# Two-layer transformer block on one core: one buffer for both feed-forward weights, reloaded per chunk, ten more probability tiles, and two scheduler constants raised

## The chip, the cores and the metric

The kernel runs on one core of one Trainium2 chip. The metric is the device time of one execution in microseconds. Every kernel was run several times, and one more execution was profiled. Engines are named as the profile names them: PE is TensorE, PEld its weight loads, DVE VectorE, ACT ScalarE, POOL GpSimd, SP SyncE with the DMA queue.

## The reference

Two attention layers (32 heads of 16) and two feed-forward layers (512 to 1376 to 512) alternate over 2,048 tokens; both attention layers use the same weights, and so do both feed-forward layers.

```python
x = A_x
x = x + _A_ref(_layernorm(x, axis=-1), A_wqkv, A_wo)
x = x + _B_ref(_layernorm(x, axis=-1), B_w1, B_b1, B_w2, B_b2)
x = x + _A_ref(_layernorm(x, axis=-1), A_wqkv, A_wo)
x = x + _B_ref(_layernorm(x, axis=-1), B_w1, B_b1, B_w2, B_b2)
# _A_ref: scores = q k^T * Dh^-0.5; p = softmax(scores); (p v) @ wo
# _B_ref: layernorm; gelu(y @ w1 + b1) @ w2 + b2
```

## The kernel before

The program is a list scheduler. Jobs written as generators hand it tasks, and when the kernel is built, a small time model in the program decides in which fixed order each engine gets its instructions. Every constant of that model can thus change the order of all that follows; this matters below.

Score tiles of 128 keys by 512 queries are made in groups, alternately three and two banks of PSUM, the memory that TensorE writes its results to. ScalarE turns a group into probabilities (exp) in slots of the tile `PT`, and a group cannot be issued before it has a slot:

```python
pl["pt3"] = Pool([0, 3, 6])     # three slots of three tiles
pl["pt2"] = Pool([9, 11])       # two slots of two tiles
...
ptn = "pt3" if gi % 2 == 0 else "pt2"
self.starved = not S_.pools[ptn].free
if self.starved:
    self.try_pv()
pt = yield ("get", ptn)
```

Some tiles go to VectorE instead, which makes exp by adding an offset to the bits (`dp`, called D tiles in the code), two tiles to a batch, with three shifted copies. A D tile needs four PV products (probabilities times V) where a ScalarE tile needs one. No new batch begins while DFLY are in flight:

```python
if self.batch is None and (not S_.pools["dp"].free or S_.pools["dp"].waiters or self.flying >= DFLY):
    return None
```

PV products are put together in bursts of one or two passes, four heads side by side. A burst is issued if its value reaches PV_LEAST, if a score group is starved for a slot, or at a segment's end (a segment is one group of four heads with one chunk of queries and a range of keys; all segments share one PSUM accumulator bank):

```python
value = lambda r: sum(min(r, len(v)) for v in by.values()) / (4.0 * (r + PV_COST))
r = max(range(1, PV_DEEP + 1), key=value)
if value(r) < PV_LEAST and not self.starved and len(near) < sg["n"] - sg["sub"]:
    return
```

The first chunk of each layer is split in two parts by keys, so that attention can begin before all keys are there. In the second layer these are eight segments of 48 tiles and eight of only 16; the segments of later full chunks have 64. Both feed-forward weights lie in buffers of their own and are loaded once, after which the key ("wld",) is marked and the small bias job starts:

```python
def bias():
    yield ("keys", [("wld",)])
    b = yield ("get", "mb")                       # takes a PSUM bank
    yield Task("pe", 3.0, [...transpose of the bias...])
    yield Task("dve", 3.0, [...copy out of the bank...])   # 3.0: a late priority
    S_.release("mb", b)
```

## Time and profile before

| | before |
|---|---|
| median time | 1733.0 us (4 runs, 1721.7 to 1734.5) |
| ScalarE busy | 1616.2 us of the 1733.2 us span |
| ScalarE exp (L1065) | 1541.0 us, 3,340 tiles |
| TensorE PV products (L1233) | 650.0 us |
| score tiles to VectorE (L1150) | 756 |
| ScalarE idle from 900 to 1120 us, the change of layers | 22.4 us |

The idle time of a stretch is its length less ScalarE's busy time in it. The prediction shows the lines.

### The profile page before, as it was taken

The numbers are of one execution on the slowest core, as the hardware profiler recorded it, in microseconds if no ns is written. First come the engines' busy times: TensorE is split into PE (matmuls) and PEld (weight loads), VectorE is DVE, ScalarE is ACT, GpSimd is POOL, SyncE is SP. The second block draws the span as 40 slices with busy tenths as digits, with TensorE's granted clock in tenths as the row PEclk, the third lists the DMA queues.
The fourth block names the chain that finished last, engine by engine and source line by source line (L and its number), as shares of the span: only waits on it lengthen the run. The fifth ranks groups of instructions, "written<-read, shape, count | busy, mean of one in ns | idle before, by whom it ended". The sixth has DMA issues, their size and how long they took to land.

```text
span 1733.2 us, 45114 instructions
## 1 busy us (share of the span) xinstructions
PE 1623.7 (94%) x19139; PEld 594.5 (34%) x19278; DVE 1383.1 (80%) x2994; ACT 1616.2 (93%) x1427; POOL 382.9 (22%) x640
## 2 busy tenths in 40 slices
PE   8989999999999999999999999999999999999998
PEld 5223323333233323233333333323233233344455
DVE  6778988868878688868888799886898879886674
ACT  3889999999999999999989898899999999999995
POOL 4145531102211122101112123411111101222310
PEclk9899999999999999999999999999999999999999
DMA  6462000001100020101541111010000100010000
GB/s 162 90 147 83 15 9 8 20 4 38 48 16 11 5 59 29 19 5 29 107 69 23 26 48 19 14 19 8 16 8 7 20 15 5 6 19 7 19 13 11
DMA packets 146446, 55.35 MB, mean 32 GB/s; under 512 B 131047, under 2 KB 140104, under 8 KB 146248
## 3 DMA queue, kind: packets, MB, share of 16 engines
q1 hardware_dynamic: 146248, 52.46, 13.9%
q8 instruction: 154, 2.52, 0.6%
q14 instruction: 44, 0.36, 0.1%
HBM read 8.69 MB, written 15.30 MB: 14 GB/s over the span
## 4 chain that ended last, share of the span: by engine, by line
PE 55%; ACT 28%; DVE 11%; issue 2%; POOL 2%; DMA 1%; DVEq 0%; POOLq 0%; another core or an unknown queue 0%; SPq 0%
ACT PT L1065 25%; PE ps L1233 18%; PE ps L1082 17%; PE ps L990 5%; PE ps L797 4%; DVE dp L1150 4%; PE ps L1351 3%; PE ps L1386 3%; DVE dp L1178 3%; PE ps L1319 3%; ACT h L1379 2%; DVE accT L1259 1%; PE ps L993 1%; POOL vs L941 1%; DMA xnT<-xn 1%
## 5 line engine op out<-in xcount | busy, mean ns | idle before, releaser
L1065 ACT ACTIVATE PT<-ps 128x1536 bf16<-128x1536 f32 (+1 forms) x1349 | 1541.0, 1258 | 84.1 <-PE ps L1082 73.9
L1150 DVE TENSOR_SCALAR dp<-ps 128x512 uint16<-128x512 f32 x756 | 511.5, 684 | 222.5 <-PE ps L1082 214.9
L1082 PE MATMUL ps<-QT,KT 32*128 32x512 bf16 (+1 forms) x4608 | 588.7, 362 | 66.0 <-DVE dp L1150 28.1
L1233 PE MATMUL ps<-PT,V 128*17 128x512 bf16 (+1 forms) x3762 | 548.2, 361 | 0.0
L941 POOL TENSOR_SCALAR vs<-V 128x340 bf16<-128x340 bf16 (+3 forms) x312 | 256.4, 828 | 916.0 <-PE ps L1233 875.4
L1178 DVE TENSOR_SCALAR dp<-dp 128x1024 uint16<-128x1024 uint16 (+1 forms) x1155 | 448.2, 433 | 4.3
L1233 PE MATMUL ps<-dp,vs 128*17 128x512 bf16 (+1 forms) x2538 | 440.2, 360 | 1.7 <-DVE dp L1178 1.7
L1082 PEld LDWEIGHTS ps<-QT,KT 32*128 32x128 bf16 x4608 | 156.4, 91 | 566.6 <-issue 211.7
L990 PE MATMUL ps<-wqkv,zw 128*32 128x256 bf16 x5864 | 256.2, 279 | 1.1 <-DVE accT L1259 1.1
L1233 PE MATMUL ps<-dp,V 128*17 128x512 bf16 (+1 forms) x846 | 213.8, 361 | 7.8 <-DVE accT L1259 6.8
L1233 PEld LDWEIGHTS ps<-PT,V 128*17 128x17 bf16 x3762 | 137.4, 88 | 136.5 <-issue 113.6
L990 PEld LDWEIGHTS ps<-wqkv,zw 128*32 128x32 bf16 x5864 | 151.2, 97 | 70.0 <-issue 48.2
L1233 PEld LDWEIGHTS ps<-dp,vs 128*17 128x17 bf16 x2538 | 118.0, 89 | 129.3 <-issue 96.5
L797 PE MATMUL ps<-wqkv,xnT 128*128 128x512 bf16 x298 | 90.0, 395 | 10.8 <-DMA xnT<-xn 5.1
L1351 PE MATMUL ps<-yT,w 128*128 128x512 bf16 (+3 forms) x361 | 91.1, 356 | 6.2 <-issue 2.9
L1386 PE MATMUL ps<-w,h 128*128 128x512 bf16 x269 | 73.2, 381 | 4.3 <-issue 3.7
L1373 DVE TENSOR_SCALAR h<-ps,b1c 128x512 bf16<-128x512 f32 (+2 forms) x88 | 62.0, 705 | 18.9 <-PE ps L1351 18.5
L1259 DVE STREAM_TRANSPOSE accT<-ps 128x512 f32<-128x512 f32 (+1 forms) x88 | 58.0, 659 | 19.0 <-PE ps L1233 13.7
L1233 PEld LDWEIGHTS ps<-dp,V 128*17 128x17 bf16 x846 | 52.0, 89 | 50.9 <-issue 19.1
L1319 PE MATMUL ps<-wo,OT 128*128 128x512 bf16 x213 | 58.9, 381 | 4.2 <-issue 3.7
L1299 DVE STREAM_TRANSPOSE OT<-ob 128x512 bf16<-128x512 bf16 (+1 forms) x72 | 46.0, 640 | 0.2
L1351 PEld LDWEIGHTS ps<-yT,w 128*128 128x128 bf16 (+1 forms) x396 | 29.5, 99 | 43.7 <-issue 18.1
(148 smaller groups left out, 747.4 us busy)
## 6 DMA issues: line engine op xcount, KB each, us to landing
q_scr<-qk SPq DMA_DIRECT2D x22, 256.0 KB, 2.0
k_scr<-qk SPq DMA_DIRECT2D x12, 256.0 KB, 2.0
out_dram<-xres SPq DMA_DIRECT2D x16, 128.0 KB, 1.7
v_scr<-vst SPq DMA_DIRECT2D x12, 136.0 KB, 1.9
V<-v_scr SPq DMA_DIRECT2D x8, 204.0 KB, 4.9
wqkv<-in_A_wqkv_dram SPq DMA_DIRECT2D x3, 512.0 KB, 5.1
q_scr<-h SPq DMA_DIRECT2D x6, 256.0 KB, 2.3
qraw<-q_scr SPq DMA_TRANSPOSE x87, 2.6
```

Source lines behind the costliest of these rows:

```text
L797: yield Task("pe", prio, [I(lambda e, c=c: e.matmul(self.ps[:, b, :], lhsT=xnT[:, c, :], rhs=self.wqkv[:, c, which * 512:which * 512 + 512 ...
L941: yield Task("pool", 0.8, [I(lambda e, k=k: e.tensor_scalar(out=self.vs[:, q, k - 1, i:i + n, :], in0=src, scalar1=WSHIFT[k], scalar2=None ...
L990: P.op("pe", lambda e, p=p: e.matmul(self.ps[p:p + 32, b, 0:w], lhsT=self.zw[:, 0:32], rhs=rhs[:, 0:w], start=st, stop=st, skip_group_chec ...
L1065: S_.submit(Task("act", 1e-5 * gi, [I(lambda e, pt=pt, n=n, b0=b0: e.activation(out=self.PT[:, pt:pt + n, :], in_=self.ps[:, b0:b0 + n, :] ...
L1082: return [I(lambda e, kb=kb, i=i: e.matmul(self.ps[:, b, i * W:(i + 1) * W], lhsT=self.KT[32 * hp:32 * hp + 32, hg, kb * 128:(kb + 1) * 12 ...
L1150: self.S_.submit(Task("dve", 0.0, [I(lambda e: e.tensor_scalar(out=self.dp[:, u, w * 512:(w + 1) * 512], in0=self.ps[:, b, :], scalar1=BIT ...
L1178: yield Task("dve", pr, [I(lambda e, k=k, v=v: e.tensor_scalar(out=self.dp[:, v, 0:N], in0=self.dp[:, u, 0:N], scalar1=float(SHIFT[k]), sc ...
L1233: ops.append((i, I(lambda e, hp=hp, v=v, ap=ap[:, i * W:(i + 1) * W], first=first and i == 0, W=W: e.matmul(self.ps[32 * hp:32 * hp + 17, ...
L1259: yield Task("dve", 0.3, [I(lambda e: e.transpose(self.accT[:, a, 0:W], self.ps[:, ACCB, 0:W]), [("ps", ACCB)], [RA], 0.15 + 0.53 * W / 512)])
L1319: yield Task("pe", pr, [I(lambda e, hg=hg, i=i, b=b: e.matmul(self.ps[:, b, :], lhsT=self.OT[:, hg, i * 128:(i + 1) * 128], rhs=self.wo[:, ...
L1351: yield Task("pe", pr, [I(lambda e, c=c: e.matmul(self.ps[0:M, b, off:off + W], lhsT=self.w1[:, c, fc * 128:fc * 128 + M], rhs=self.yT[:, ...
L1386: yield Task("pe", pr, [I(lambda e, fc=fc, i=i, b=b: e.matmul(self.ps[:, b, :], lhsT=self.gt(fc, i, W), rhs=self.w2[:, fc, :], start=(fc = ...
```

## The change

The intent: keep only one of the two feed-forward weights on the chip at a time, reload both for each chunk of tokens, and use the freed space for probability slots, so that exp can run further ahead and PV products can wait until full bursts of eight are together. In the second layer the second weights lie in the buffer of the QKV weights, which are no longer needed then.

```diff
-DFLY = 3
+DFLY = 4
...
-PV_LEAST = 0.6
+PV_LEAST = 0.75
...
-        self.w1 = t("w1", [128, 4, self.F], BF16)
-        self.w2 = t("w2", [128, NFC, 512], BF16)
+        self.wf = t("wf", [128, NFC, 512], BF16)
...
-        self.PT = t("PT", [128, 13, 512], BF16)
+        self.PT = t("PT", [128, 23, 512], BF16)
...
-        pl["pt3"] = Pool([0, 3, 6])
-        pl["pt2"] = Pool([9, 11])
+        pl["pt3"] = Pool([0, 3, 6, 13, 18])
+        pl["pt2"] = Pool([9, 11, 16, 21])
...
-            (the loads of w1 and w2 in the start-up job)
             S_.mark(("wld",))
...
+        yield ("keys", [("kv", 1, tt) for tt in range(self.NT)] + [("wld",)])
+        for qc in range(self.NC + 1):
+            L = 1 if qc < self.NC else 3
+            if qc:
+                yield ("keys", [("post", 1, qc - 1)])
+            for fc in range(self.NFC):
+                yield first(fc)
+                S_.mark(("w1", L, qc % self.NC, fc))
+            if L == 1:
+                for fc in range(self.NFC):
+                    yield ("keys", [("w1u", 1, qc, fc)])
+                    yield from second(1, fc)
+                    S_.mark(("w2", 1, qc, fc))
... (matmuls and waits take the new names; the second layer loads both weights once)
```

More of the change, by code (lines that the diff above doesn't have):

```diff
@@ L687, in fills @@
             yield f(lambda e: e.memset(self.bst[:, :], 0.0), [("bst",)], 0.3)
-            yield f(lambda e: e.memset(self.w2[:, nfull, :], 0.0), [("w2z",)], 0.6)
+            yield f(lambda e: e.memset(self.wf[:, nfull, :], 0.0), [("wf", nfull)], 0.6)
             yield f(lambda e: e.memset(self.g10[:, :], 0.0), [("g10",)], 0.6)
@@ L699, in fills @@
                 yield ld(lambda e, hp=hp: e.dma_start(self.wo[32 * hp:32 * hp + 16, :, :], wor[hp]), [("wo0",)], [("wo", hp)])
-            w1r = self.B_w1.rearrange("(c p) n -> p c n", p=128)
-            for c in range(4):
-                yield ld(lambda e, c=c: e.dma_start(self.w1[:, c, :], w1r[:, c, :]), [], [("w1", c)])
-            w2r = self.B_w2[0:nfull * 128, :].rearrange("(c p) n -> p c n", p=128)
-            for c in range(0, nfull, 5):
-                yield ld(lambda e, c=c: e.dma_start(self.w2[:, c:c + 5, :], w2r[:, c:c + 5, :]), [], [("w2", c // 5)])
-            yield ld(lambda e: e.dma_start(self.w2[0:self.FLAST, nfull, :], self.B_w2[nfull * 128:self.F, :]), [("w2z",)], [("w2", 2)])
-            yield ld(lambda e: e.dma_start(self.w2[96:97, nfull, :], self.B_b2.rearrange("(o n) -> o n", o=1)), [("w2z",)], [("w2", 3)])
             S_.mark(("wld",))
         S_.spawn(fills(), 4.0)
+        S_.spawn(self.flow_weights(), 2.0)
         def bias():
@@ L717, in build_startup_late, with w1, w2, w2res @@
         S_.spawn(bias(), 3.0)
+    def w1(self, fc, c):
+        M = 128 if fc < self.NFC - 1 else self.FLAST
+        return self.wf[:, fc, c * M:(c + 1) * M]
+    def w2(self, L, fc):
+        if L == 1:
+            return self.wf[:, fc, :]
+        return self.wqkv[:, :, :].rearrange("p c n -> p (c n)")[:, fc * 512:(fc + 1) * 512]
+    def w2res(self, L, fc):
+        return [("wf", fc)] if L == 1 else [("w2", fc)]
+    def flow_weights(self):
+        S_ = self.S_
+        nf = self.NFC - 1
+        wr1 = self.B_w1.rearrange("(c p) n -> p c n", p=128)
+        ld = lambda fn, writes: self.dma(fn, [], writes, 2.0, 0.1, 4.0)
+        def first(fc):
+            M = 128 if fc < nf else self.FLAST
+            dst = self.wf[:, fc, 0:4 * M].rearrange("p (c m) -> p c m", m=M)
+            return ld(lambda e: e.dma_start(dst, wr1[:, :, fc * 128:fc * 128 + M]), [("wf", fc)])
+        def second(L, fc):
+            W = self.w2res(L, fc) + ([("wqkv", fc % 3)] if L == 3 else [])
+            M = 128 if fc < nf else self.FLAST
+            yield ld(lambda e: e.dma_start(self.w2(L, fc)[0:M, :], self.B_w2[fc * 128:fc * 128 + M, :]), W)
+            if fc == nf:
+                yield ld(lambda e: e.dma_start(self.w2(L, fc)[M:M + 1, :], self.B_b2.rearrange("(o n) -> o n", o=1)), W)
+        yield ("keys", [("kv", 1, tt) for tt in range(self.NT)] + [("wld",)])
[6 more added lines that the diff above has]
+                S_.mark(("w1", L, qc % self.NC, fc))
+            if L == 1:
+                for fc in range(self.NFC):
+                    yield ("keys", [("w1u", 1, qc, fc)])
+                    yield from second(1, fc)
+                    S_.mark(("w2", 1, qc, fc))
+        yield ("keys", [("kd", 3, tt) for tt in range(self.NT)])
+        for fc in range(self.NFC):
+            yield from second(3, fc)
+            S_.mark(("w2", 3, 0, fc))
+        for qc in range(1, len(self.units[3])):
+            for fc in range(self.NFC):
+                S_.mark(("w1", 3, qc, fc))
+                S_.mark(("w2", 3, qc, fc))
     def ln_group(self, tiles, slot, prio, eps1, eps0):
@@ L837, in job_qkv_tile @@
             S_.release("mb", b)
+        S_.mark(("kd", L, tt))
         if not start:
@@ L1346, in job_yt, with mm_w1 @@
         S_.mark(("yt", L, tt))
-    def mm_w1(self, fc, b, pr, W, off=0):
+    def mm_w1(self, L, qc, fc, b, pr, W, off=0):
         M = 128 if fc < self.NFC - 1 else self.FLAST
+        yield ("keys", [("w1", L, qc, fc)])
         for c0 in (0, 2):
-            yield Task("pe", pr, [I(lambda e, c=c: e.matmul(self.ps[0:M, b, off:off + W], lhsT=self.w1[:, c, fc * 128:fc * 128 + M], rhs=self.yT[:, c, 0:W], start=(c == 0), stop=(c == 3)),
-                                    [("w1", c)] + [("yT", i) for i in range(W // 128)], [("ps", b)], 0.216 * W / 512, [("ps", b)]) for c in (c0, c0 + 1)])
+            yield Task("pe", pr, [I(lambda e, c=c: e.matmul(self.ps[0:M, b, off:off + W], lhsT=self.w1(fc, c), rhs=self.yT[:, c, 0:W], start=(c == 0), stop=(c == 3)),
+                                    [("wf", fc)] + [("yT", i) for i in range(W // 128)], [("ps", b)], 0.216 * W / 512, [("ps", b)]) for c in (c0, c0 + 1)])
     def gt(self, fc, i, W):
@@ L1369, in job_ffn @@
             M = 128 if fc < nf else self.FLAST
-            yield ("ready", "pe", [("yT", i) for i in range(len(tiles))])
+            yield ("keys", [("w1", L, qc, fc)])
+            yield ("ready", "pe", [("yT", i) for i in range(len(tiles))] + [("wf", fc)])
             b = yield ("get", "mb")
-            yield from self.mm_w1(fc, b, pr, W)
+            yield from self.mm_w1(L, qc, fc, b, pr, W)
+            S_.mark(("w1u", L, qc, fc))
             S_.submit(Task("dve", pr - 0.7, [I(lambda e, fc=fc, M=M, b=b: e.tensor_scalar(out=hv[0:M, fc * W:(fc + 1) * W], in0=self.ps[0:M, b, 0:W], scalar1=self.b1c[0:M, fc:fc + 1], scalar2=None, op0=ALU.add),
@@ L1381, in job_ffn @@
         GR = HR + [("g10",)]
+        yield ("keys", [("w2", L, qc, fc) for fc in range(NFC)])
         for i, tt in enumerate(tiles):
-            yield ("ready", "pe", GR)
+            yield ("ready", "pe", GR + [r for fc in range(NFC) for r in self.w2res(L, fc)])
             b = yield ("get", "mb")
             for f0 in range(0, NFC, 2):
-                yield Task("pe", pr, [I(lambda e, fc=fc, i=i, b=b: e.matmul(self.ps[:, b, :], lhsT=self.gt(fc, i, W), rhs=self.w2[:, fc, :], start=(fc == 0), stop=(fc == nf)),
-                                        GR + [("w2", k) for k in range(4)], [("ps", b)], 0.216, [("ps", b)]) for fc in range(f0, min(f0 + 2, NFC))])
+                yield Task("pe", pr, [I(lambda e, fc=fc, i=i, b=b: e.matmul(self.ps[:, b, :], lhsT=self.gt(fc, i, W), rhs=self.w2(L, fc), start=(fc == 0), stop=(fc == nf)),
+                                        GR + self.w2res(L, fc), [("ps", b)], 0.216, [("ps", b)]) for fc in range(f0, min(f0 + 2, NFC))])
             S_.submit(Task("dve", pr - 0.7, [I(lambda e, tt=tt, b=b: e.tensor_tensor(out=self.xres[:, tt, :], in0=self.ps[:, b, :], in1=self.xres[:, tt, :], op=ALU.add), [("ps", b), ("x", tt)], [("x", tt)], 0.68)]),
@@ L1425, in second @@
             GR = [("gt", fc)]
-            yield Task("pe", pr - 0.1, [I(lambda e, i=i: e.matmul(self.ps[:, acc[i], :], lhsT=self.gt(fc, i, W), rhs=self.w2[:, fc, :], start=(fc == 0), stop=(fc == nf)),
-                                          GR + [("w2", k) for k in range(4)], [("ps", acc[i])], 0.216, [("ps", acc[i])]) for i in range(n)])
+            yield ("keys", [("w2", L, qc, fc)])
+            yield Task("pe", pr - 0.1, [I(lambda e, i=i: e.matmul(self.ps[:, acc[i], :], lhsT=self.gt(fc, i, W), rhs=self.w2(L, fc), start=(fc == 0), stop=(fc == nf)),
+                                          GR + self.w2res(L, fc), [("ps", acc[i])], 0.216, [("ps", acc[i])]) for i in range(n)])
             if fc == nf:
@@ L1436, in job_tail @@
             b = yield ("get", "mb")
-            yield from self.mm_w1(fc, b, pr, W)
+            yield from self.mm_w1(L, qc, fc, b, pr, W)
             dst = self.gv[:, fc * W:(fc + 1) * W] if fc < nf else self.g10[0:M, 0:W]
```

## The prediction

> **What bounds the kernel now.** I read the page's engine table first, then the slices, the costliest groups (also with the shapes kept apart), the table of stretches, and last a few microseconds of the timeline.
>
> ```profile
> PE 1623.7 (94%) x19139; PEld 594.5 (34%) x19278; DVE 1383.1 (80%) x2994; ACT 1616.2 (93%) x1427; POOL 382.9 (22%) x640
> L1065 ACT ACTIVATE PT<-ps 128x1536 bf16<-128x1536 f32 (+1 forms) x1349 | 1541.0, 1258 | 84.1 <-PE ps L1082 73.9
> L1150 DVE TENSOR_SCALAR dp<-ps 128x512 uint16<-128x512 f32 x756 | 511.5, 684 | 222.5 <-PE ps L1082 214.9
> L990 PE MATMUL ps<-wqkv,zw 128*32 128x256 bf16 x5864 | 256.2, 279 | 1.1 <-DVE accT L1259 1.1
> ```
>
> PE's 94% is not a bound: the group on L990, 5,864 matmuls, is filler put into gaps to keep the clock up (its result is used nowhere). ScalarE is. Its exp group alone is 1541.0 us, and only 84.1 us of idle time stand before it. The table of stretches shows how little is left:
>
> ```profile
> 0.00:125.00 125.00, 112.19 (x930) 45.10 (x941) 87.32 (x207) 83.33 (x91) 44.00 (x122) 0.89 0.61 134
> 200.00:900.00 700.00, 660.25 (x7196) 221.85 (x7256) 562.31 (x1190) 678.61 (x586) 129.25 (x184) 0.99 0.14 30
> 900.00:1120.00 220.00, 206.06 (x2491) 73.99 (x2497) 192.54 (x415) 197.60 (x176) 65.50 (x121) 0.98 0.12 26
> 1120.00:1680.00 560.00, 529.63 (x7015) 201.56 (x7061) 452.44 (x986) 550.56 (x473) 100.17 (x95) 1.00 0.06 12
> 1680.00:1734.00 54.00, 46.55 (x697) 27.82 (x705) 21.75 (x50) 34.89 (x38) 1.52 (x4) 1.00 0.03 11
> ```
>
> The fourth busy column is ScalarE: 678.61 of 700 and 550.56 of 560. Of its 117 us idle, 42 lie before 125 us and 19 after 1680 us (start and tail, which the change doesn't touch); 22 lie from 900 to 1120, where the second attention layer waits for the first one's feed-forward part; some 35 are small gaps elsewhere. So the time can fall in two ways: those gaps, or fewer tiles for ScalarE. The second exists because a score tile (128x512) can go either to ScalarE, or to VectorE, which makes exp by bit arithmetic (one eviction on L1150, then three shifted copies on L1178, two tiles to a copy), at the price of four PV products in place of one.
>
> Unit costs. ScalarE: 642 groups of three tiles and 707 of two are 3,340 tiles, 1541.0 / 3340 = 0.461 us each. VectorE, for a tile of its own: 684 ns plus 3 x 438 / 2 ns = 1.34 us (438 ns is the mean of the 1024-wide copies with shapes kept apart). VectorE is 80% busy and waits 214.9 us for scores to evict, so it has room.
>
> **What the Trainium skill says.** "ScalarE: Activation LUTs", What ACT_TABLE_LOAD costs: an ACTIVATE with immediate scale and bias takes 186 ns + 0.833 N, and back-to-back ones overlap by 93 ns. For N = 1536 and 1024 that is 1466 and 1039 ns; the trace has 1482 and 1054. So exp runs at its floor, and buffers cannot make a tile cheaper. "TensorEngine Tiling (Array Packing)", Key Properties: changing the tiling mode drains TensorE. Scores are row-tiled and PV products column-tiled, so each PV burst pays it. The trace agrees:
>
> ```profile
> 702.86 0.09 PEld L1233 LDWEIGHTS ps<-PT,V 128*17 128x17 bf16 x1 [0.23 <-issue]
> ...
> 703.18 0.10 PEld L1082 LDWEIGHTS ps<-QT,KT 32*128 32x128 bf16 x3 [0.23 <-PE ps L1082]
> ...
> 704.94 0.09 PEld L1233 LDWEIGHTS ps<-dp,V 128*17 128x17 bf16 x1 [0.23 <-DVE dp L1150]
> ...
> 705.50 0.13 PEld L1082 LDWEIGHTS ps<-QT,KT 32*128 32x128 bf16 x3 [0.46 <-PE ps L1082]
> ```
>
> A burst of one pass (four products side by side) occupies 0.32 us from its start to the next scores, one of two passes 0.56 us: 0.08 us fixed and 0.24 us a pass. "DMA: Bandwidth & Descriptors", Specifications: transfers under 512 B miss line rate. The new first-weight loads come in 256-byte rows; no run yet shows what that costs.
>
> **The change part by part.** The instruction order is fixed when the program is built, so its decisions, though not their times, can be counted from the kernel before. I counted them: 1,574 PV bursts, 1,056 of one pass and 518 of two, 545 of them forced because no probability slot was free; 403 of the 1,349 score groups met an empty slot pool, 387 of these the pool of two slots; and 208 times a new VectorE batch was refused because three were in flight, in 187 of which a PSUM bank was free.
>
> *PV_LEAST 0.6 to 0.75.* The value of a burst is (tiles) / 4(r + 0.5) with r passes. One full pass is 0.67, two passes with six, seven and eight tiles are 0.6, 0.7 and 0.8. So only full bursts of eight pass now, apart from forced ones and ends of segments. *Ten more tiles* (five slots of three and four of two, from three and two) are what allows waiting for eight. Today's 3,340 + 4 x 756 = 6,364 PV tiles need 796 full bursts; with an odd one for each of 88 segments, some 900 of about 1,720 passes. Saved on TensorE: 670 x 0.08 + (2,092 - 1,720) x 0.24 = 143 us. Nearly all lies beside ScalarE and will turn into filler and idle time. What pays is a score group that no longer comes late. Outside start and tail ScalarE idles 57 us; the 22 us of the layer transition are mostly data not yet computed, so I take about a quarter: 15 us.
>
> *DFLY 3 to 4.* The 187 refusals bring far fewer new batches: a refusal with three in flight mostly means that VectorE is behind with its copies, and the next try a microsecond later succeeds. One in eight, two tiles each, is about 45 more tiles. On VectorE, 45 x 1.34 = 60 us, beside the path (to about 85%). TensorE gets 135 more PV tiles, 34 passes, 8 us, paid from the 143. ScalarE loses 45 x 0.461 = 21 us, on the path.
>
> *Shared weight buffer.* It frees 128x4x1376 bf16, 11,008 B a partition, for ten tiles of 1,024 B. It adds some 107 DMA issues and 11.3 MB (five loads of 2.8 MB in place of one), against 55.35 MB now and a mean DMA load of 32 GB/s. First weights are reloaded once the chunk before is through, about a chunk's attention (some 190 us) ahead; second weights when their column's first product is issued, behind the rest of those products, a 4.5 us gelu and table loads, against 4 to 6 us to landing for today's weight loads. Hidden; I count 0.
>
> Sum: 1733.9 - 15 - 21 = 1698; I say 1697 us.
>
> **Rivals.** *Only ScalarE's floor.* If no more tiles go to VectorE, at most small gaps close: 1715 to 1728, same. For it: 98% busy from 1120 to 1680 us. Against: the refusals counted, and VectorE's 215 us of waiting. *VectorE fills up.* If most refusals turn into batches, 110 more tiles put VectorE at 1383 + 147 = 1530 us, still below the span, and save 51 us; with 20 us of gaps, 1663. Against: the refusals come when it is behind; and 708 other refusals, for want of a PSUM bank, remain. *Large bursts block scores.* A burst holds TensorE 0.56 us, and a two-tile exp lasts about 0.95 us, of which the next scores need some 0.4 with their wait. If 850 bursts cost 0.04 us each, 34 us are lost and the gain is gone: 1730. For it: ScalarE waits on scores already; against: 518 two-pass bursts run today at 97% ScalarE. *Weights come late.* A stall of 4 us in the chunk from 900 to 1120 us, the one on the path, or a reload held up in the in-order DMA queue, adds 4 to 10 us, no more, since the other chunks' feed-forward runs beside attention.
>
> **Range and chances.** The centre is 36 us below, almost exactly the 2% line (1699). The floor rival and the blocking rival pull up, the VectorE rival down. 80%: 1662 to 1727. Faster by over 2%: 0.52; within 2%: 0.44; slower: 0.04, since no part of it puts more than some 10 us on the path.
>
> **What would show it.** PV: unbroken runs of L1233 matmuls, 1,100 now at a mean of 6.5, fall below 900. L1150 rises from 756 to about 800 and L1065's busy time falls by about 20 us to 1520. ScalarE's idle time between 125 and 1680 us falls from 57 to about 42. Filler on L990 rises above 5,864. VectorE goes to about 85%. No wait on a weight load appears among the longest. Wrong if L1150 stays at 756, if ScalarE's idle time before L1065 grows (blocking), or if feed-forward matmuls wait for DMA.

## The result, and the profile after

The changed kernel took 1707.5 us in the median (4 runs, 1704.4 to 1710.4) against 1733.0 us; all runs were fast ones. Ratios are the mean time of one kernel's fast runs over that of the other's of the same rounds, so they are not quite the ratio of the medians: here 0.9866, with a 95% interval from 0.9819 to 0.9913. Repeated later beside other kernels it was 0.9891 (0.9871 to 0.9911). The time lies in the predicted range, but the gain is 1.1 to 1.3%, not 2.1%.

One figure has to be held beside every comparison below: the granted TensorE clock that each run lists. In each kernel's own fast runs the time goes with it (correlation -0.88 to -0.99), by 1.0 to 1.5 us for each 0.001; the 54 runs of the kernel before in the last rounds reach from 1741.6 us at 0.982 to 1721.7 us at 0.993. The traces show the clock at 0.50 in short stretches, often 3.4 or 6.8 us long, and at 1.00 between them. The changed kernel's median clock in its repeat was 0.9835, that of the kernel before 0.989. At the same clock the gain is thus larger: at 0.985 one run of 1705.7 us stands against 1734.7 and 1736.5 us. What lowers the clock was not tested.

The engine table and the costliest groups of the profile after (line, engine and operation, count, busy time and mean, idle time before):

```profile
PE 1585.4 (93%) x19711; PEld 568.6 (33%) x19711; DVE 1374.4 (80%) x3011; ACT 1609.6 (94%) x1426; POOL 378.5 (22%) x640
L1110 ACT ACTIVATE PT<-ps 128x1536 bf16<-128x1536 f32 (+1 forms) x1348 | 1534.3, 1262 | 67.0 <-PE ps L1127 61.3
L1195 DVE TENSOR_SCALAR dp<-ps 128x512 uint16<-128x512 f32 x758 | 510.2, 682 | 208.4 <-PE ps L1127 200.7
L1035 PE MATMUL ps<-wqkv,zw 128*32 128x256 bf16 x6152 | 241.5, 280 | 1.1 <-DVE accT L1304 1.1
```

L1110 answers to L1065 of before, L1195 to L1150, L1035 to L990. VectorE got 758 tiles for 756, so nothing moved away from ScalarE. What fell is the idle time before exp, from 84.1 to 67.0 us, and with it the busy time, by 6.7 us, though a group's mean did not shorten. The span fell by 24.6 us: 18.0 us less idle time on ScalarE and 6.6 us less busy time.

The table of stretches says where (columns as before: after the stretch come PE, PEld, DVE, ACT and POOL busy, clock and DMA):

```profile
200.00:900.00 700.00, 657.02 (x7644) 214.17 (x7640) 566.01 (x1216) 682.99 (x593) 125.72 (x184) 0.99 0.18 42
900.00:1120.00 220.00, 202.48 (x2473) 69.93 (x2465) 189.73 (x414) 209.40 (x188) 67.18 (x123) 0.99 0.19 46
1120.00:1680.00 560.00, 524.60 (x7529) 201.26 (x7530) 454.99 (x999) 549.53 (x474) 97.53 (x92) 0.99 0.06 13
```

From 900 to 1120 us ScalarE is busy for 209.40 us where it was for 197.60; the two long stretches change by 4.4 and -1.0 us. Counted by exp tiles instead of time, the changed kernel is 7.5 us ahead at its 1,700th tile (which before ended at 884 us) and 22.8 us ahead at its 2,100th (1,100 us); after that it only keeps its lead.

The waits of ScalarE around that stretch (895 to 1120 us; engine and what it waited for, us in total, times, longest), first before, then after:

```profile
ACT PT L1065 <- PE ps L1082: 22.9, 20, 3.6
```

```profile
ACT PT L1110 <- PE ps L1127: 9.5, 18, 1.8
```

One of the waits of before, in the order of time (start, duration, engine and line):

```profile
1078.93 1.48 PE L1233 MATMUL ps<-PT,V 128*17 128x512 bf16 x7
...
1080.20 1.06 PE L1233 MATMUL ps<-dp,vs 128*17 128x512 bf16 x2
...
1081.20 1.03 PE L1082 MATMUL ps<-QT,KT 32*128 32x512 bf16 x5
...
1081.87 2.37 ACT L1065 ACTIVATE PT<-ps 128x1024 bf16<-128x1024 f32 x2 [3.60 <-PE ps L1082]
```

Here a new segment could only begin its PV products once the accumulator of the last one had been read (the transpose on L1259, from 1077.53 us for 0.71 us); those products ran from 1078.5 to 1081.3 us, the next scores started at 1081.20, and exp had sat idle for 3.60 us. This wait, the longest of the stretch, is not a clean example, since the clock was 0.50 from 1075.8 to 1082.6 us. But it does not stand alone. Of the waits of exp over 0.25 us from 900 to 1120 us, 21.6 us in all, eight with 15.8 us end within 4 us after an accumulator was read, seven of them at full clock; after, it is six with 6.3 us of 7.9 us. From 200 to 900 us, with 28 such reads to the 16 here, the same count gives 2.5 us before and 1.0 us after. Reading the schedule as it was built, 57 of the 163 groups of these sixteen short segments found their slot pool empty before, and 16 of 167 after. Over the whole kernel it was 403 of 1,349 and 66 of 1,348.

TensorE's busy time on PV products (the table of stretches with that line alone) fell as predicted, though the time hardly did. Before:

```profile
0.00:1734.00 1734.00, 650.00 (x7146) 179.08 (x7146) 0.99 0.15 32
```

After:

```profile
0.00:1709.00 1709.00, 521.52 (x7179) 136.36 (x7179) 0.98 0.17 39
```

The first figure after the stretch is PE: 128.5 us less for much the same products (7,179 recorded for 7,146; the schedule has only six PV tiles more, and some records are missing).

### The profile page after: what moved, and what is told of

It is laid out like the page before. It is cut to its first block, busy times and chain, and to the rows that moved or that the text cites. A ratio compares the mean times of both kernels' runs of the same rounds, so it can differ in the third digit from the quotient of the medians.

```text
span 1708.6 us, 46394 instructions
## 1 busy us (share of the span) xinstructions
PE 1585.4 (93%) x19711; PEld 568.6 (33%) x19711; DVE 1374.4 (80%) x3011; ACT 1609.6 (94%) x1426; POOL 378.5 (22%) x640
## 4 chain that ended last, share of the span: by engine, by line
PE 47%; ACT 40%; DVE 8%; POOL 2%; issue 2%; DMA 1%; SPq 0%; DVEq 0%; POOLq 0%
ACT PT L1110 37%; PE ps L1127 15%; PE ps L1278 13%; PE ps L1035 4%; PE ps L841 4%; PE ps L1397 4%; DVE dp L1195 3%; PE ps L1364 3%; PE ps L1435 3%; ACT h L1427 2%; DVE dp L1223 2%; POOL vs L986 1%; DVE accT L1304 1%; PE ps L1038 1%; ACT L1110 1%
## 5 line engine op out<-in xcount | busy, mean ns | idle before, releaser
L1110 ACT ACTIVATE PT<-ps 128x1536 bf16<-128x1536 f32 (+1 forms) x1348 | 1534.3, 1262 | 67.0 <-PE ps L1127 61.3
L1127 PE MATMUL ps<-QT,KT 32*128 32x512 bf16 (+1 forms) x4608 | 604.2, 363 | 108.5 <-ACT PT L1110 43.8
L1195 DVE TENSOR_SCALAR dp<-ps 128x512 uint16<-128x512 f32 x758 | 510.2, 682 | 208.4 <-PE ps L1127 200.7
L1278 PE MATMUL ps<-PT,V 128*17 128x512 bf16 (+1 forms) x3751 | 469.7, 363 | 0.4 <-DVE accT L1304 0.4
L1278 PE MATMUL ps<-dp,vs 128*17 128x512 bf16 (+1 forms) x2571 | 397.3, 359 | 0.0
L1035 PE MATMUL ps<-wqkv,zw 128*32 128x256 bf16 x6152 | 241.5, 280 | 1.1 <-DVE accT L1304 1.1
L1278 PE MATMUL ps<-dp,V 128*17 128x512 bf16 (+1 forms) x857 | 201.4, 364 | 3.0 <-DVE accT L1304 2.9
L1035 PEld LDWEIGHTS ps<-wqkv,zw 128*32 128x32 bf16 x6152 | 144.5, 97 | 93.3 <-issue 76.0
L1278 PEld LDWEIGHTS ps<-PT,V 128*17 128x17 bf16 x3751 | 114.7, 88 | 91.1 <-issue 73.7
L1278 PEld LDWEIGHTS ps<-dp,vs 128*17 128x17 bf16 x2571 | 101.9, 89 | 85.3 <-issue 71.4
L1397 PE MATMUL ps<-yT,wf 128*128 128x512 bf16 (+3 forms) x396 | 98.5, 359 | 0.5 <-DVE h L1421 0.3
L906 POOL TENSOR_TENSOR qt<-n,qy 128x32 f32<-128x32 f32 x32 | 11.1, 347 | 160.1 <-DVE qy L902 159.6
L1397 PEld LDWEIGHTS ps<-yT,wf 128*128 128x128 bf16 (+1 forms) x396 | 29.5, 99 | 46.5 <-issue 18.6
```

The source lines that it names most:

```text
L1035: P.op("pe", lambda e, p=p: e.matmul(self.ps[p:p + 32, b, 0:w], lhsT=self.zw[:, 0:32], rhs=rhs[:, 0:w], start=st, stop=st, skip_group_chec ...
L1110: S_.submit(Task("act", 1e-5 * gi, [I(lambda e, pt=pt, n=n, b0=b0: e.activation(out=self.PT[:, pt:pt + n, :], in_=self.ps[:, b0:b0 + n, :] ...
L1127: return [I(lambda e, kb=kb, i=i: e.matmul(self.ps[:, b, i * W:(i + 1) * W], lhsT=self.KT[32 * hp:32 * hp + 32, hg, kb * 128:(kb + 1) * 12 ...
L1195: self.S_.submit(Task("dve", 0.0, [I(lambda e: e.tensor_scalar(out=self.dp[:, u, w * 512:(w + 1) * 512], in0=self.ps[:, b, :], scalar1=BIT ...
L1278: ops.append((i, I(lambda e, hp=hp, v=v, ap=ap[:, i * W:(i + 1) * W], first=first and i == 0, W=W: e.matmul(self.ps[32 * hp:32 * hp + 17, ...
L1397: yield Task("pe", pr, [I(lambda e, c=c: e.matmul(self.ps[0:M, b, off:off + W], lhsT=self.w1(fc, c), rhs=self.yT[:, c, 0:W], start=(c == 0 ...
```

## The experiments

The questions: is it the slots, the bursts, DFLY, or the reload that does it; and where do the slots pay? The first four kernels do one part alone or undo one, with five rounds each, beside the kernel before (1727.9 us in these rounds, 19 runs).

**Weights only (e1).** The changed kernel, with all other parts undone:

```diff
-DFLY = 4
+DFLY = 3
-PV_LEAST = 0.75
+PV_LEAST = 0.6
-        pl["pt3"] = Pool([0, 3, 6, 13, 18])
-        pl["pt2"] = Pool([9, 11, 16, 21])
+        pl["pt3"] = Pool([0, 3, 6])
+        pl["pt2"] = Pool([9, 11])
```

> The changed kernel with only the shared, reloaded weight buffer left of it: five probability slots, DFLY 3 and PV_LEAST 0.6 as before. If the reload is hidden, as predicted: within 0.4% of before, 1727 to 1740 us, and the second layer's start (900 to 1120 us) as idle on ScalarE as before, about 22 us. If the reload itself is what brings part of the gain, or costs: below 1725 or above 1742 us.

Measured: 1749.3 us, 1.0112 of before (1.0089 to 1.0134). That was a miss: the reload seemed to cost 19 us. But the stretch at the change of layers is as before (22.6 us idle). The loss is one gap. The timeline of this kernel from 103 to 137 us:

```profile
104.01 0.17 PE L706 MATMUL ps<-ident,bst 32*128 32x32 bf16 x1
...
134.73 0.15 DVE L707 CAST b1c<-ps 128x11 f32<-128x11 bf16 x1
134.92 0.63 PE L1127 MATMUL ps<-QT,KT 32*128 32x512 bf16 x7
135.37 2.37 ACT L1110 ACTIVATE PT<-ps 128x1024 bf16<-128x1024 f32 x2 [29.41 <-PE ps L1127]
```

The bias is transposed into a PSUM bank at 104.01 us, and its copy out of the bank, at the late priority 3.0, comes 30.7 us later. As the copy ends, seven score matmuls start, and exp ends a gap of 29.41 us. In the code, the first score groups of five banks wait until each bank has been given up by the small jobs. The changed kernel marks ("wld",) before the large loads, not after them, so the bias job now starts just when those banks are being collected. In the kernel before, its transpose ran at 129.1 us, when that was over, and took 3.0 us with its copy.

**Slots only (e2).** As e1, but with the ten tiles and their slots.

```diff
-DFLY = 4
+DFLY = 3
-PV_LEAST = 0.75
+PV_LEAST = 0.6
```

> Shared weights and the ten tiles more, but DFLY 3 and PV_LEAST 0.6. Buffer theory (the slots let exp run on over the ends of segments, most where these are short, at the start and at the change of layers): nearly the whole gain, 1705 to 1715 us, ScalarE idle from 900 to 1120 us at most 13 us. Burst theory (it is TensorE time saved by large bursts that pays): at most a third of the gain, 1724 us or more.

Measured: 1732.8 us, 1.0018 of before (1.0003 to 1.0034). By its time this is the burst theory's case (1724 us or more), but the time decides nothing, since this kernel has the same gap as e1 (29.3 us, its bias copy 30.6 us late). It is 16.5 us faster than e1, and idles 17.8 us from 900 to 1120 us, where the buffer theory said at most 13.

**DFLY undone (e3).** The changed kernel with `DFLY = 3`.

> The changed kernel with DFLY 3. Counted in its schedule, 747 tiles go to VectorE in place of 758. If DFLY 4 brings these 11 tiles and no more: 11 x 0.461 = 5 us slower than the changed kernel, about 1712 us. If it does nothing: 1707 us. If it carries the gain: 1720 us or more.

Measured: 1719.8 us, 0.9948 of before (0.9929 to 0.9967). Half of the gain is gone, nearly the 1720 us set for "it carries the gain" and more than eleven tiles explain (747 went to VectorE, as counted). Its idle time at the change of layers is 15.4 us. The last experiment shows why this difference may not be read as DFLY's worth.

**Bursts only (e4).** The kernel before with `PV_LEAST = 0.75`.

> The kernel before with PV_LEAST 0.75 and nothing else. Counted in its schedule, bursts fall only from 1574 to 1393, and those forced by want of a slot rise from 545 to 962. Burst theory: some gain, 1715 to 1725 us. Buffer theory: none, since a pool of five slots can't wait for eight; 1730 to 1745 us.

Measured: 1749.4 us, 1.0105 of before (1.0078 to 1.0131): no gain, and somewhat worse than the buffer theory said. Larger bursts without slots make exp wait: from 900 to 1120 us ScalarE is busy for 188.79 us, so it idles 31.2 us there.

In the second four the two bias instructions got early priorities, so that the gap of e1 cannot hide the rest (before: 1727.4 us in these rounds, 55 runs):

```diff
-            yield Task("pe", 3.0, [...transpose of the bias...])
-            yield Task("dve", 3.0, [...copy out of the bank...])
+            yield Task("pe", 0.3, [...transpose of the bias...])
+            yield Task("dve", -1.0, [...copy out of the bank...])
```

**Weights only, bias mended (e5).** e1 with this edit.

> The weights-only kernel of the first four runs, with only the priority of the two bias instructions raised (their transpose and its copy out of a PSUM bank). There the copy came 30.7 us after its transpose and held a bank that the five-bank score groups waited for: one idle gap of 29.4 us on ScalarE. Bias theory (the reload itself costs nothing, the late copy of its earlier-freed bias job does): the gap goes to about 6 us, the time to 1.0112 - 23/1728 = 0.998 of before, about 1724 us. Rival (the reload's DMA costs the 19 us): still above 1742 us.

Measured: 1734.8 us, 1.004 of before (1.0025 to 1.0055), between the numbers of the two theories (1724 us, and over 1742). The waits from 95 to 140 us, in e1 and then here:

```profile
ACT PT L1110 <- PE ps L1127: 31.1, 3, 29.4
```

```profile
ACT PT L1110 <- PE ps L1127: 11.5, 5, 8.8
```

The gap went from 29.4 to 8.8 us and the copy follows its transpose after 0.8 us. The median fell by 14.5 us, the profiled span by 22.3 (the profiled run of e1 was its slowest, at a clock of 0.985; that of e5 had 0.991). So the late copy is the larger part of e1's loss; what stays, 0.4%, is within what a new order of instructions does by itself (see the last experiment), and no trace shows a feed-forward matmul that waits for weights.

**Slots only, bias mended (e6).** e2 with this edit.

> The pool-only kernel with the same two priorities raised. Bias theory: 1.0018 - 23/1728 = 0.9885 of before, about 1708 us, the time of the changed kernel without either of its other constants; so the ten tiles alone would be worth about 16 us over the weights-only kernel with the same mend. If the tiles don't pay by themselves: 1722 us or more.

Measured: 1723.5 us, 0.9966 of before (0.9952 to 0.9981), 11.3 us faster than e5. The absolute number was missed: 1723.5 us lies in the range set for tiles that don't pay by themselves (1722 us or more). The difference is two thirds of the 16 us expected. The stretch from 900 to 1120 us, in e5 and then in e6:

```profile
900.00:1120.00 220.00, 205.20 (x2507) 72.65 (x2504) 188.09 (x406) 193.98 (x174) 64.15 (x121) 1.00 0.20 45
```

```profile
900.00:1120.00 220.00, 204.81 (x2550) 72.38 (x2542) 188.56 (x408) 205.71 (x183) 69.41 (x123) 1.00 0.20 45
```

ScalarE idles 26.0 and 14.3 us. That is 11.7 of the 18.4 us by which its whole idle time differs in these two traces (121.5 and 103.1 us); their spans differ by 15.7 us, at the same clock of 0.991.

**All parts, bias mended (e7).** The changed kernel with this edit.

> The changed kernel with the same two priorities raised. In it the copy also came late, 13.6 us after its transpose, but ScalarE's gap there is 6.2 us as in the kernel before. If that gap is the bank's: up to 6 us less, 1700 to 1704 us. If it is the score data's: 1707 us as it was.

Measured: 1721.5 us, 0.995 of before (0.9935 to 0.9964). So PV_LEAST 0.75 and DFLY 4 together bring 2.0 us over e6, with overlapping intervals, although TensorE's time on PV products is 524.9 us here and 609.9 in e6. But the clock was lower as well, 0.980 in the median for 0.989. At the one clock that both reached, 0.986, e6 took 1726.6 and 1727.6 us and e7 1714.6 us. So 85 us saved on TensorE were worth 2 us as the kernels ran, and some 12 us at the same clock (one run against two), of which eight tiles fewer for ScalarE (766 on VectorE for 758) are an estimated 4. The kernels with nine slots and PV_LEAST 0.75 (the changed one, e3, e7, e9, e12) had median clocks from 0.980 to 0.985, all others from 0.9855 to 0.9905; whether the larger bursts are the reason was not tested. And this kernel, though its bias can hold nothing up, is 12 us slower than the changed kernel without the edit in its repeat (1709.3 us; 10 us by the ratios, and its clock is lower, 0.980 for 0.9835), a miss that neither theory foresaw. The gap at 108 us is 8.4 us here, so in the changed kernel it was not the bank's.

**Five slots (e8).** e7 with the slots back at five, and the larger bursts kept.

```diff
-        pl["pt3"] = Pool([0, 3, 6, 13, 18])
-        pl["pt2"] = Pool([9, 11, 16, 21])
+        pl["pt3"] = Pool([0, 3, 6])
+        pl["pt2"] = Pool([9, 11])
```

> The same as the run before, with the probability slots back at five (thirteen tiles used) and PV_LEAST 0.75 and DFLY 4 kept. Counted in its schedule: 1395 bursts, 784 tiles to VectorE in place of 766. Buffer theory: large bursts without slots hold exp back, 1730 to 1750 us, as with bursts only (1749). If more tiles to VectorE outweigh that (18 x 0.461 = 8 us): 1700 to 1710 us.

Measured: 1746.7 us, 1.011 of before (1.0078 to 1.0141), 25 us slower than e7, from which it differs in the slots alone. The slots are needed for the bursts, even with 784 tiles on VectorE. Idle from 900 to 1120 us: 29.2 us.

The last four (before: 1729.0 us in these rounds, 54 runs) ask whether the result holds, where the slots pay, and what luck is worth.

**The changed kernel again (e9).** No edit.

> The changed kernel once more, unedited, beside the kernels below and on the chip that they run on: the first comparison had four runs of each and an interval from 0.982 to 0.991. If the first result holds: 0.984 to 0.991 of before. If part of it was that comparison's few runs: 0.991 to 0.995, the same as with DFLY 3 (0.9948) and with the bias mended (0.995).

Measured: 1709.3 us, 0.9891 of before (0.9871 to 0.9911). The result holds.

**Slots at the change of layers only (e10), and everywhere else (e11).** e6, with the ten tiles' slots opened when the schedule reaches the second layer's first segment and closed after its sixteenth, or the other way about:

```diff
+                while self.slot_at and self.cur >= self.slot_at[0][0]:
+                    ... release, or retire, slots 13 and 18 of "pt3", 16 and 21 of "pt2"
+        self.slot_at = [(40, True), (56, False)]      # e10; e11: [(40, False), (56, True)]
```

> The pool kernel with the bias mended (DFLY 3, PV_LEAST 0.6), its extra slots open only for the 16 short segments with which the second layer begins. In the traces that kernel leads the weights-only one by 4 us or less at the 1,700th tile and by 17 us at the 2,100th. If the slots pay at the change of layers alone: as the pool kernel, 0.996 to 0.999 of before. If they pay everywhere: near the weights-only kernel, 1.002 to 1.004.

> The mirror of the run before: the extra slots open everywhere but in those 16 segments. If the slots pay at the change of layers alone: as the weights-only kernel, 1.002 to 1.006. If they pay everywhere: 0.997 to 1.000.

Measured: e10 1734.4 us, 1.0039 (1.0023 to 1.0055); e11 1732.7 us, 1.0013 (0.9997 to 1.0029). Taken by the whole time, e10 misses the range of "at the change of layers alone" and falls in that of "everywhere" (1.002 to 1.004), while e11 falls between its two ranges. So the whole time speaks against the theory that the slots pay at the change of layers. The stretch itself agrees with it. In e10, then in e11:

```profile
900.00:1120.00 220.00, 198.87 (x2461) 71.88 (x2473) 188.29 (x406) 202.41 (x181) 68.36 (x121) 0.98 0.20 45
```

```profile
900.00:1120.00 220.00, 205.33 (x2621) 76.18 (x2622) 191.75 (x413) 191.09 (x170) 66.50 (x121) 0.96 0.19 45
```

ScalarE idles 17.6 us with the slots open there and 28.9 us with five, though a part of that is the clock: it stood at 0.50 for 6.8 us of the stretch in e10 and for 17.1 us in e11. Counted by tiles the same shows: between its 1,700th and 2,100th exp tile, that is over the change of layers, e10 gains 10.1 us on the kernel before and e6, with slots everywhere, 10.0 us, while e11 loses 9.3 us and e5 3.4 us. But e10 gives its gain back later: from 1120 to 1680 us it idles 18.9 us where e6 idles 13.7, and 3,345 tiles fall to ScalarE in place of 3,338 (7 x 0.461 = 3.2 us).

**A change that means nothing (e12).** The changed kernel with another constant of its model nudged:

```diff
-PV_NEAR = 0.7
+PV_NEAR = 0.71
```

> The changed kernel with PV_NEAR 0.71 in place of 0.7, a change that should mean nothing by itself but lays the instruction lists out anew (929 bursts for 939, 745 tiles to VectorE for 758). What it differs by from the unedited kernel is how much of any of these differences may be the luck of a schedule. If schedules hardly matter: within 0.2% of it. If they do: 0.4% or more, and the shares of DFLY and of the bursts can't be told apart from luck.

Measured: 1728.5 us, 0.9998 of before (0.9983 to 1.0014), 19 us slower than the unedited kernel of the same rounds. That is as large as the gain of the whole change, and little of it is the clock: at 0.983, e9 took 1709.5 and 1711.1 us, e12 1726.2 to 1729.7. The exp group and VectorE's evictions, in e9 and then in e12:

```profile
L1110 ACT ACTIVATE PT<-ps 128x1536 bf16<-128x1536 f32 (+1 forms) x1348 | 1534.1, 1266 | 68.2 <-PE ps L1127 62.7
L1195 DVE TENSOR_SCALAR dp<-ps 128x512 uint16<-128x512 f32 x758 | 510.4, 683 | 207.3 <-PE ps L1127 199.9
```

```profile
L1110 ACT ACTIVATE PT<-ps 128x1536 bf16<-128x1536 f32 (+1 forms) x1353 | 1540.6, 1269 | 73.9 <-PE ps L1127 68.8
L1195 DVE TENSOR_SCALAR dp<-ps 128x512 uint16<-128x512 f32 x745 | 502.1, 683 | 220.6 <-PE ps L1127 214.5
```

Thirteen tiles more fell to ScalarE (13 x 0.461 = 6.0 us), and it idled 107.1 us in place of 100.1: with 0.7 us more of other work, nearly the 13.8 us by which the profiled spans differ, at clocks of 0.983 and 0.984. From 900 to 1120 us it idles 16.0 us, still as a kernel with slots does.

## Why the prediction was right or wrong

**The bound: right.** ScalarE set the time. The changes of its idle and busy time, 18.0 and 6.6 us, make up the 24.6 us of the span.

**Larger bursts: right in size; that they lie beside the path is not settled.** The count of bursts in the schedule fell to 939 (900 predicted), unbroken runs of PV matmuls from 1,100 to 762 (below 900), and TensorE's PV time by 128.5 us (143 predicted). The prediction's unit costs hold: 635 bursts fewer at 0.08 us and 331 passes fewer at 0.24 us (the schedule's 1,761 for 2,092) are 130 us. That the 0.08 us is a drain is not shown, only that there is a fixed part. e6 and e7 show what the bursts pay with DFLY 4: 2 us for 85 us on TensorE, with the lower clock that came along; some 12 us at the same clock, eight tiles moved to VectorE included. The prediction had no place for the clock.

**Idle time on ScalarE: right in size, wrong in place.** Between 125 and 1680 us it fell from 57 to 43 us (42 predicted). But the working said "the 22 us of the layer transition are mostly data not yet computed" and expected the gain in the small gaps elsewhere. In fact 11.8 us of it came at that transition. What the runs put in its place: with five slots the short segments there hold exp back. The six traces with five slots in this stretch (before, e1, e4, e5, e8, e11) idle 22.4 to 31.2 us from 900 to 1120 us, the eight with nine slots (after, e2, e3, e6, e7, e9, e10, e12) 10.6 to 18.1 us. The two sets don't overlap, and their means, 26.7 and 15.2 us, differ by 11.5 us. The clock is not the reason: without the idle time that falls at a clock of 0.50 they are 18.6 to 28.5 and 8.4 to 14.3 us. Counted between the 1,700th and 2,100th tile they nearly touch (20.9 to 32.4, and 8.1 to 20.6 us). In the long segments an empty pool was met as often (some 30% of the groups of each 64-tile chunk) and cost nothing that shows. The reason is likely the shared accumulator at the segments' ends: the waits from 900 to 1120 us that end within 4 us after it was read make 9.5 to 22.0 us in the six traces and 3.7 to 8.4 us in the eight. No run changed the accumulator, so this is not shown by an experiment.

Closing a gap also shortened exp's busy time, which the prediction had not counted: start to start, back-to-back groups of three tiles take 1,331 ns in the trace (median), though one lasts 1,457 ns (median), because neighbours overlap. There are 1,138 overlapping pairs after, 1,099 before, and their overlaps sum to 167.3 and 156.1 us. These 11.2 us, less 4.5 us by which the groups themselves lasted longer in sum, are the 6.7 us. So exp's busy time per tile did fall a little (0.4614 to 0.4597 us), which the prediction ruled out.

**DFLY: wrong.** This is the step that failed, "one in eight, two tiles each, is about 45 more tiles", worth 21 us. VectorE got two more tiles: the prediction's own sign of being wrong, "if L1150 stays at 756", came true, VectorE stayed at 80% (85% predicted), and exp's busy time fell to 1534.3 us, not 1520. The filler rose as predicted, to 6,152 matmuls. In the schedule, refusals because of DFLY fell from 208 to 65, but others took their place: no free `dp` unit 100 times (9 before), the VectorE queue too long 185 (108), two loads under way 178 (140); want of a bank stayed at 718 (708). With 12 units and four to a batch, three batches already fill the pool if PV products that wait for full bursts still hold them; this is read from the code and these counts. DFLY 4 in the changed kernel is counted to bring 11 tiles (758 for 747), an estimated 5 us. Take these 21 us from the sum of 36 and 15 remain; the 6.7 us of overlap and 3 us more of idle time make up the rest. So the time came near the range's centre in part by luck: one term failed and another, not foreseen, replaced a third of it; and the nudged kernel (e12, 1728.5 us), with the same mechanism, would have missed the range. (The sums of the prediction hold; after 1680 us ScalarE idles 18 us rather than 19, since the span ends at 1733.2.)

**The reload: right in itself.** No wait for a weight load is in the trace's list of waits; the loads landed after 3.1 us (first weights) and 2.0 us (second). But the change had a side effect that the prediction didn't look for: the bias job started earlier and could hold a PSUM bank. It cost e1 and e2 a gap of 29 us. In the changed kernel the copy was 13.6 us late, at a gap of 6.2 us, as long as that of before, and e7 shows nothing to be gained there.

**The rivals.** The one of large bursts that block scores came true only without slots (e4, e8). "Only ScalarE's floor" was nearest: no tile moved, and the time fell below its 1715 us because the transition was no floor.

**What stays open.** How much of the 1.1 to 1.3% belongs to the idea and how much to this one order of instructions. The slots' effect at the change of layers shows in every pair of traces that differ there in the slots alone: 11 to 12 us of idle time in three (e5 and e6, e8 and e7, e11 and e10), 4.9 us in e1 and e2. Beyond it the kernels with slots lie between 0.987 and 1.004 of before, and a nudge without meaning moved the changed kernel by 19 us. So the shares of DFLY (e3), of the larger bursts, of the mended bias in e7 and of the reload's remaining 0.4% (e5) are not settled by these runs. e10 and e11 failed to show the local gain in the whole time, perhaps for the same reason. No version tried beats the changed kernel.

## What to carry to other kernels

Buffers pay where work comes in short pieces with a hand-over between them: look for the idle time of the bounding engine by stretch, and don't take a stretch for data-bound before more slots have been tried there. Time saved on an engine beside the path can be worth little (2 us for 85 us of TensorE here), but look at the granted clock of both kernels before you say so (some 12 us at the same clock, tiles moved included). A cap that is raised passes its refusals on to the next cap, so count all of them. When the program's own scheduler fixes the order, run a meaningless nudge as a control before you credit a per cent to a constant, and see that no low-priority job holds a bank that the main loop is about to collect.

## What the Trainium skill lacked or had wrong

- "ScalarE: Activation LUTs", What ACT_TABLE_LOAD costs, gives 93 ns of overlap for back-to-back ACTIVATEs. Here consecutive exp groups out of PSUM overlap by 127 ns in the median and 147 ns in the mean (profile after), so, as an estimate, a gap between two groups costs that much on top of its length.
- "TensorEngine Tiling (Array Packing)", Key Properties, says that a change of tiling mode drains TensorE, but not what it costs. Here, worked out from two bursts of the timeline, the fixed part of a burst, which may be that drain, is about 0.08 us beside 0.24 us a pass.
- "DMA: Bandwidth & Descriptors", Specifications, sets 512 B as the least transfer for line rate, and the page gives no time to landing for a load in shorter rows on this queue. Here 128 KB in rows of 256 B landed after 3.1 us in the median (2.2 to 5.0), 128 KB in rows of 1,024 B after 2.0 us (1.8 to 3.5). The first were issued eleven in a row, so the rows alone are not shown to be the cause.
- No page has a word on the luck of a fixed order of instructions: an edit without meaning moved this kernel from 1709.3 to 1728.5 us.
